# New planned times, a charge for changes to f32r products, and scores and transposes planned four at a time

## The chip, the cores and the metric

The kernel runs on one core of a Trainium2 chip. The metric is the device time of one execution in microseconds. A core has five engines that run side by side, each with its own queue of instructions: TensorE (PE: matrix products and transposes; PEld is its weight load), VectorE (DVE), ScalarE (ACT), GpSimd (POOL) and SyncE (SP, which here only starts DMAs). Each engine works through its queue in order; an instruction that has to wait for another engine holds up what is queued behind it.

## The reference

Three computations follow each other. The first is a gated linear attention with a complex decay over 768 steps, for 4 batches, 8 heads and 48 dimensions; the second a two-layer network with a leaky activation on the 3072 x 384 result; the third a mixture of 8 experts.

```
scale = min(mag, 0.999) / (mag + 1e-6)           # mag = |a|; a = a * scale
for t in range(768):                              # attention, per batch and head
    S = a[t][:, None] * S + k[t][:, None] * v[t][None, :]     # S complex, 48 x 48
    y[t] = q[t] @ real(S)
x = y as 3072 x 384
h = x @ w_in                                      # 384 -> 2048
g = max(h, 0) + alpha * min(h, 0)
x = g @ w_out                                     # 2048 -> 384
out = x                                           # where x @ w_skip <= 0
e = argmax(x @ w_gate); p = softmax(x @ w_gate)[e]            # elsewhere, 8 experts
out = x + p * (relu(x @ w1[e]) @ w2[e])           # 384 -> 1024 -> 384
```

## The kernel before

The sequence of tokens is cut into 24 sub-chunks of 128 tokens. For each sub-chunk `s`, `elementwise` (label `E`) normalises the decay on ScalarE and VectorE in tiles of 128x384 called X and Rr (logarithm, exponential, arctangent, sine, prefix scans), and writes the modulated q and k through DRAM into the tiles qh and kh. `attention` (label `P`) then makes on TensorE, in fp32:

- the scores at<-qh,kh, two groups of four heads (parts `a` and `b`), which VectorE masks into A;
- the transposes at<-ident,kh of kh, two groups of four (parts `t`, `u`), which ScalarE copies to kT;
- the outputs y<-A,vt and y<-qh,St (part `y`), the state update sps<-vt,kT (part `s`), which VectorE puts into St;
- the split of y into two f32r parts (part `h`): xhi, a cast on ScalarE, and xlo = y - xhi on VectorE.

`moe_block` (label `M`) takes two sub-chunks at a time, 256 tokens, so there are 12 blocks. Each has 8 pairs of hidden tiles: 18 products h<-xhi/xlo,wih/wil of 256 columns per pair; the activation hs; its parts gh (a cast on ScalarE) and gl (VectorE); and 12 products acc<-woh/wol,gh/gl of 394 columns. Products of f32r parts (hi x hi, hi x lo, lo x hi) stand for one fp32 product. The weights w_in and w_out come as 64-bit words and are decoded in the first 115 us (`decode`, labels `d`: raw, Ai and Ao on VectorE, then wih, wil, woh, wol). The second network's nine items (labels `I`, weights w1h, w1l, w2h, w2l) gather the tokens of an expert by DMA (xg), transpose them (xt<-ident,xg) and split them again into xhi and xlo before their h products. Filler products (h<-ident, fp32) keep TensorE busy between 27 and 55 us of the plan, where it waits.

The order is not the order of the code. Each operation is recorded in a `Plan` with an engine, a planned cost, what it reads and writes, and a planned time from the table `WHEN` (L55 on, tenths of a unit, one number for each operation of a label and part). `Plan.emit` then simulates the engines in time: on each engine it takes, of the operations that are ready in the simulation, the one with the lowest planned time, and adds its cost; the resulting order on each engine is what is emitted. It also places ScalarE's table loads (L1080), one for each change between the set of Ln/Exp and that of Arctan/Sin, and lets an operation of the loaded set go first if its planned time is within `stick` of the other. So a cost in the planner changes the order of everything behind it, and no instruction by itself.

In the trace, L1151 is `mm` (a single product), L1156 `transpose`, L1430 `columns` (a list of products planned as one operation), L1108 `act`, L1113 `copy`, L1120 `tt`, L1128 `stt`, L1139 `scan`. Before the change, the four scores of a group are four `mm` operations, and the four transposes are four `transpose` operations, each with its own planned time:

```
for x in range(4):
    mm(at[:, x * 128:(x + 1) * 128], kh[:, 4 * g + x, 0:128], qh[0:96, 4 * g + x, :], True, True)
```

Of the kernel before, what the change touches and what calls it, by code (L numbers as in the profile page):

```python
# [55 lines left out]
    "d": "764",  # L56
    "E0x": "28 237",
    "E0e": "191 90 98 104 146 172 122 58 111 168 179 168 176 89 100 175 178 190 213 191 200 204 217 165 229 238 "
        "312 177 217",
    "E0k": "179 283 281 403",  # L60
    "E0q": "502 478 626",
    "d0ir": "142",
    "d0i": "128 168 -3 28 -47",
    "d0or": "-301",
    "d0o": "256 265 332 397 409 661 496 285 458 269 458 453",
    "d1ir": "171",
    "d1i": "227 220 234 292 301",
    "d1or": "180",
    "d1o": "192 201 213 302 290 397 276 221 142 251 317 341",
    "E1x": "159 268",  # L70
    "E1e": "129 152 175 154 131 156 192 182 213 251 195 293 253 353 321 287 316 279 396 305 318 325 356 327 363 "
        "359 385 409 381",
    "E1k": "223 221 247 393",
    "E1q": "409 410 459",
    "P0v": "620",
    "P0a": "447 459 457 464 468",
    "P0b": "471 452 475 479 482",
    "P0t": "719 844 855 859 762",
    "P0u": "589 571 491 583 535",
    "P0y": "412",  # L80
    "P0s": "574 643",
    "P0h": "108 -31",
    "d2ir": "163",
    "d2i": "235 148 283 352 361",
    "d2or": "317",
    "d2o": "281 254 302 395 364 417 503 392 391 387 382 321",
    "d3ir": "272",
    "d3i": "24 -48 -81 -60 -36",
    "d3or": "208",
    "d3o": "347 355 360 275 429 364 360 386 475 272 288 269",  # L90
    "P1v": "290",
    "P1a": "376 425 296 307 315",
    "P1b": "490 478 481 479 491",
    "P1t": "639 638 662 773 609",
    "P1u": "764 769 873 804 837",
    "P1y": "741",
    "P1s": "628 973",
    "P1h": "481 497",
    "E2x": "247 288",
    "E2e": "343 295 299 393 394 484 436 520 459 427 462 491 470 544 385 491 561 563 645 592 569 589 620 697 624 "  # L100
        "716 708 724 719",
    "E2k": "665 720 490 777",
    "E2q": "828 747 894",
    "E3x": "447 919",
    "E3e": "384 490 455 398 539 664 586 589 588 600 642 669 658 655 732 736 759 830 881 777 825 835 852 893 862 "
        "891 877 902 906",
    "E3k": "961 949 876 961",
    "E3q": "798 648 808",
    "d4ir": "602",
    "d4i": "383 455 454 561 516",  # L110
    "d4or": "424",
    "d4o": "458 464 452 531 476 526 501 569 501 539 588 532 517",
    "d5ir": "-85",
    "d5i": "450 420 448 442 498",
    "d5or": "117",
    "d5o": "368 274 259 163 277 280 272 262 162 246 243 271 466",
    "d6ir": "481",
    "d6i": "557 562 538 605 598",
    "d6or": "859",
    "d6o": "499 508 541 572 506 562 651 626 625 392 385 431 563",  # L120
    "d7ir": "255",
    "d7i": "607 577 652 686 693",
    "d7or": "782",
    "d7o": "638 640 663 668 640 679 695 665 680 671 679 657 689",
    "d8ir": "340",
    "d8i": "670 686 600 709 673",
    "d8or": "508",
    "d8o": "667 707 683 741 732 729 678 685 725 743 752 746 728",
    "d9ir": "583",
    "d9i": "736 715 733 739 767",  # L130
    "d9or": "593",
    "d9o": "677 700 675 678 678 685 685 686 681 686 686 685 707",
    "P2v": "821",
    "P2a": "905 921 931 935 912",
    "P2b": "804 815 822 790 801",
    "P2t": "742 720 746 746 797",
    "P2u": "1013 1001 952 1015 1083",
    "P2y": "686",
    "P2s": "1098 1258",
    "P2h": "1061 1168",  # L140
    "d10ir": "853",
    "d10i": "745 764 770 774 835",
    "d10or": "619",
    "d10o": "819 811 825 854 834 862 877 863 883 893 918 896 935",
    "d11ir": "782",
    "d11i": "802 807 829 870 857",
    "d11or": "823",
    "d11o": "876 872 861 904 894 896 974 932 988 879 1041 940 899",
    "d12ir": "708",
    "d12i": "885 919 931 968 934",  # L150
    "d12or": "817",
    "d12o": "866 864 849 864 867 934 879 1055 968 1017 955 923",
    "P3v": "1119",
    "P3a": "1118 1088 1072 1047 1113",
    "P3b": "1057 1093 1056 1094 1124",
    "P3t": "1141 1142 1144 1143 1223",
    "P3u": "1079 1111 1114 1115 1141",
    "P3y": "810",
    "P3s": "1235 1610",
    "P3h": "1219 1172",  # L160
    "d13ir": "1157",
    "d13i": "966 1006 1003 869 815",
    "d13or": "1145",
    "d13o": "994 919 984 1029 1020 1017 924 1060 1083 1089 1075 895",
    "d14ir": "924",
    "d14i": "728 768 763 901 816",
    "d14or": "981",
    "d14o": "676 664 706 699 709 709 690 715 660 707 692 857",
    "d15ir": "946",
    "d15i": "1079 1084 1066 1132 1121",  # L170
    "d15or": "1535",
    "d15o": "1087 1069 1114 1111 1119 1112 1220 1166 1137 1174 1165 1167",
    "M0.0": "412 415 425 417 396 432 410 440 430 395 417 417 287 308 290 342 327 308 295 296 327 368 376",
    "M0.1": "617 643 664 651 675 659 646 656 650 614 668 597 674 674 690 707 699 699 712 713 704 724 748 668 702 "
        "750 710 720 679 808 720 744 738 766 768",
    "M0.2": "676 675 680 679 666 678 682 693 669 678 672 678 660 707 702 697 708 719 823 760 782 814 785 792 747 "
        "759 759 779 663 640 668 624 672 598 673",
    "M0.3": "696 617 667 720 717 580 616 589 601 616 639 650 647 633 654 658 637 658 674 713 634 712 728 653 655 "
        "627 658 664 677 659 689 696 677 695 739",
    "M0.4": "802 818 802 811 822 821 815 811 804 801 818 816 824 789 834 718 845 901 895 847 915 859 993 854 871 "  # L180
        "896 892 961 960 898 937 914 794 812 855",
    "M0.5": "849 845 849 833 849 855 823 871 900 879 885 877 879 865 886 910 886 885 992 955 959 1018 1016 989 "
        "1015 1018 992 975 962 1064 1020 1028 981 965 989",
    "M0.6": "973 998 985 1009 1004 976 1012 999 950 1017 952 993 1016 1044 1014 1005 1040 1020 1017 988 1023 1094 "
        "1054 1058 1001 969 968 984 1011 1054 1057 1023 1051 1070 1099",
    "M0.7": "1022 1035 1019 1048 1091 1047 1066 1068 1085 1112 1129 1091 1074 1061 1083 1108 1102 1118 1110 1123 "
# [24 lines left out]
    "E4k": "1335 1386 1217 1623",  # L211
    "E4q": "1286 1423 1381",
    "P4v": "1604",
    "P4a": "1469 1428 1430 1433 1444",
    "P4b": "1458 1405 1322 1316 1325",
    "P4t": "1529 1521 1540 1498 1508",
    "P4u": "1434 1435 1337 1297 1320",
# [2035 lines left out]
```

## Time and profile before

| | before |
|---|---|
| median of 3 runs | 747.38 us (747.15 to 749.46) |
| profiled execution | 749.78 us, of which the span of instructions is 747.8 us |
| TensorE busy | 703.7 us (94%), 7290 instructions |
| VectorE busy | 596.0 us (80%), 1401 instructions |
| ScalarE busy | 507.1 us (68%), 869 instructions, 83 of them profiled table loads of 1283 ns |
| GpSimd busy | 95.8 us (13%) |
| granted TensorE clock | 0.999 |

The span is 747.8 us; the rest of the execution lies around the first and last instruction. Busy shares over the span hide the stages: up to 60 us TensorE mostly waits for the decoded weights and the first attention outputs; from 60 to 617 us the first network's blocks and the attention of later sub-chunks share the engines; from 617 us the experts' items run; after 741 us only the last output is written. So each reading below is of one stretch. In a list of instructions in time, a record's duration is longer than the engine's time for it, since products are pipelined: the engine's time is the distance from one start to the next. A fp32 product shows as two records (x2), one for each of its passes.

### The profile page before, as it was taken

The numbers are of one execution on the slowest core, as the hardware profiler recorded it, in microseconds if no ns is written. First come the engines' busy times: TensorE is split into PE (matmuls) and PEld (weight loads), VectorE is DVE, ScalarE is ACT, GpSimd is POOL, SyncE is SP. The second block draws the span as 40 slices with busy tenths as digits, with TensorE's granted clock in tenths as the row PEclk, the third lists the DMA queues.
The fourth block names the chain that finished last, engine by engine and source line by source line (L and its number), as shares of the span: only waits on it lengthen the run. The fifth ranks groups of instructions, "written<-read, shape, count | busy, mean of one in ns | idle before, by whom it ended". The sixth has DMA issues, their size and how long they took to land.

```text
span 747.8 us, 18414 instructions
## 1 busy us (share of the span) xinstructions
PE 703.7 (94%) x7290; PEld 670.6 (90%) x7290; DVE 596.0 (80%) x1401; ACT 507.1 (68%) x869; POOL 95.8 (13%) x154
## 2 busy tenths in 40 slices
PE   0589999999999999999999999999999998999996
PEld 0478989889999999999989999999999998999996
DVE  7999999899988999899888899965465473886623
ACT  6779669799999888899889777632222362565411
POOL 5000000101201102010120100201010304502111
PEclk9999999999999999999999999999999999999999
DMA  8595862648654646365354957576543544799300
GB/s 292 157 288 191 265 204 72 150 136 234 168 136 117 205 131 181 105 179 172 95 125 143 244 175 229 159 185 190 154 138 118 162 157 145 243 396 396 118 16 19
DMA packets 84685, 130.64 MB, mean 175 GB/s; under 512 B 8822, under 2 KB 60096, under 8 KB 84592
## 3 DMA queue, kind: packets, MB, share of 16 engines
q1 hardware_dynamic: 79152, 111.19, 50.0%
q0 software_dynamic: 5440, 18.21, 7.8%
q8 instruction: 59, 0.97, 0.5%
q14 instruction: 34, 0.28, 0.1%
HBM read 99.46 MB, written 31.29 MB: 175 GB/s over the span
## 4 chain that ended last, share of the span: by engine, by line
PE 44%; DVE 17%; issue 14%; ACT 11%; DMA 10%; POOL 2%; SPq 1%; POOLq 0%; DVEq 0%; ACTq 0%
PE acc L1151 18%; PE h L1151 18%; ACT X L1108 4%; ACT L1080 4%; PE at L1151 3%; DVE X L1120 3%; PE y L1430 3%; DMA X<-in_a 3%; DVE X L1128 2%; DVE X L1139 2%; DMA raw<-in_w_out 2%; DMA qh<-qd 1%; DVE gl L1120 1%; DMA rawc<-in_w_out 1%; DMA lst<-tok,ix 1%
## 5 line engine op out<-in xcount | busy, mean ns | idle before, releaser
L1151 PE MATMUL h<-xhi,wih 128*128 128x256 f32 x576 | 163.0, 289 | 2.6 <-DVE hs L1120 1.2
L1151 PE MATMUL h<-xlo,wih 128*128 128x256 f32 x576 | 162.5, 286 | 0.2
L1151 PE MATMUL h<-xhi,wil 128*128 128x256 f32 x576 | 161.3, 285 | 0.0
L1108 ACT ACTIVATE X<-X 128x384 f32<-128x384 f32 (+1 forms) x216 | 119.0, 560 | 27.8 <-DVE X L1139 9.9
L1151 PE MATMUL acc<-woh,gh 128*128 128x394 f32 x384 | 134.1, 357 | 1.1 <-ACT gh L1113 1.1
L1151 PE MATMUL acc<-woh,gl 128*128 128x394 f32 x384 | 129.5, 348 | 1.3 <-DVE gl L1120 1.1
L1151 PE MATMUL acc<-wol,gh 128*128 128x394 f32 x384 | 129.8, 345 | 0.0
L1151 PEld LDWEIGHTS h<-xhi,wih 128*128 128x128 f32 x576 | 108.6, 190 | 5.9 <-ACT hs L1113 1.9
L1151 PEld LDWEIGHTS h<-xlo,wih 128*128 128x128 f32 x576 | 109.0, 190 | 1.2 <-DVE xlo L1120 0.9
L1151 PEld LDWEIGHTS h<-xhi,wil 128*128 128x128 f32 x576 | 108.9, 190 | 0.5 <-issue 0.4
L1080 ACT ACT_TABLE_LOAD x83 | 106.5, 1283 | 1.5
L1113 ACT CAST gh<-hs 128x512 fp32r<-128x512 f32 x96 | 58.3, 617 | 45.1 <-PE acc L1151 31.0
L1120 DVE TENSOR_TENSOR X<-X 128x384 f32<-128x384 f32 (+1 forms) x96 | 71.7, 750 | 13.4 <-ACT X L1108 12.9
L1120 DVE TENSOR_TENSOR gl<-hs,gh 128x512 fp32r<-128x512 f32 x96 | 65.0, 684 | 19.1 <-ACT gh L1113 18.7
L1151 PEld LDWEIGHTS acc<-woh,gh 128*128 128x128 f32 x384 | 71.6, 189 | 5.0 <-ACT gh L1113 3.0
L1128 DVE SCALAR_TENSOR_TENSOR hs<-hs,alp 128x256 f32<-128x256 f32 x144 | 62.1, 478 | 16.8 <-ACT hs L1113 16.6
L1151 PEld LDWEIGHTS acc<-woh,gl 128*128 128x128 f32 x384 | 71.6, 189 | 3.7 <-DVE gl L1120 2.9
L1151 PEld LDWEIGHTS acc<-wol,gh 128*128 128x128 f32 x384 | 72.5, 189 | 0.3 <-issue 0.2
L1113 ACT COPY hs<-h 128x512 f32<-128x512 f32 x72 | 40.1, 582 | 39.1 <-PE h L1151 33.4
L1612 POOL DMA_INDIRECT lst<-tok,ix x24 | 31.0, 1291 | 242.0 <-DVE ix L1124 227.7
L1151 PE MATMUL at<-qh,kh 96*128 96x128 f32 x384 | 54.6, 277 | 2.4 <-DMA qh<-qd 2.4
L1151 PEld LDWEIGHTS at<-qh,kh 96*128 96x128 f32 x384 | 49.8, 191 | 3.8 <-issue 2.2
(191 smaller groups left out, 1370.7 us busy)
## 6 DMA issues: line engine op xcount, KB each, us to landing
r<-in_w SPq DMA_DIRECT2D x24, 512.0 KB, 8.4
r<-in_w SPq DMA_DIRECT2D x32, 384.0 KB, 8.6
kd<-QP SPq DMA_DIRECT2D x24, 387.0 KB, 4.9
kh<-kd SPq DMA_DIRECT2D x24, 387.0 KB, 5.7
qd<-X SPq DMA_DIRECT2D x24, 384.0 KB, 3.2
qh<-qd SPq DMA_DIRECT2D x24, 384.0 KB, 5.0
X<-in_a POOLq DMA_DIRECT2D x18, 384.0 KB, 6.3
X<-in_qk POOLq DMA_DIRECT2D x18, 384.0 KB, 6.9
```

The source lines that it names most:

```text
L1080: nc.scalar.preload_act_table_set(o)
L1108: lambda: nc.scalar.activation(real(o), real(i), f, **{k: real(x) for k, x in kw.items()}),
L1113: lambda: nc.scalar.copy(real(o), real(i)), [i], [o])
L1120: dve(o, cols(o), lambda: nc.vector.tensor_tensor(out=real(o), in0=real(x), in1=real(y), op=op), [x, y], late=late)
L1128: dve(o, cols(o), lambda: nc.vector.scalar_tensor_tensor(out=real(o), in0=real(x), scalar=real(s), in1=real(y), op0=op0, op1=op1), [x, y, s])
L1139: dve(o, 2 * cols(o) - 16, lambda: nc.vector.tensor_tensor_scan(out=real(o), data0=real(x), data1=real(y), initial=real(init), op0=ALU.mul ...
L1151: pl.add("PE", cost / 1e3, lambda: nc.tensor.matmul(real(o), lhsT=real(l), rhs=real(r), start=start, stop=stop, skip_group_check=True), [l ...
L1430: ins = nc.tensor.matmul(real(o), lhsT=real(l), rhs=real(r), start=alone or first and n < 4, stop=alone or n >= len(ops) - 4, skip_group_c ...
L1612: r = nc.gpsimd.indirect_dma_start(out=lst, out_offset=bass.IndirectOffsetOnAxis(ap=real(ix[:, t:t + 1].bitcast(U32)), axis=0), in_=toks[t ...
```

## The change

Four things change, none of them in what is computed.

- An operation has a new field `swift`, true for f32r products (`mm` sets it). In the simulation of `Plan.emit`, a swift operation on TensorE that follows one that is not swift costs `swap` = 0.085 us more.
- The four scores of a group become one `columns` operation with a planned cost of 4 x 0.223 us, in place of four of their own.
- The four transposes of a group become one operation with a planned cost of 0.36 us.
- All numbers of `WHEN` are new; parts a, b, t and u have two numbers for each sub-chunk in place of five (four products and the operation behind them).

```
-    "P9a": "2306 2347 2382 2361 2409",
+    "P9a": "2371 2614",
...
-    def add(self, eng, cost, fn, reads=(), writes=(), after=(), lag=0.0, table=None, late=0.0):
+    def add(self, eng, cost, fn, reads=(), writes=(), after=(), lag=0.0, table=None, late=0.0, swift=False):
...
-        o.label, o.part = self.label, self.part
+        o.label, o.part, o.swift = self.label, self.part, swift
...
             if e == "PE":
+                cost += self.swap * (o.swift and not swift)
+                swift = o.swift
...
-    stick = 10
+    stick, swap = 10, 0.085
...
-               [l, r] + ([] if start else [o]), [o])
+               [l, r] + ([] if start else [o]), [o], swift=dt == F32R)
...
-                for x in range(4):
-                    mm(at[:, x * 128:(x + 1) * 128], kh[:, 4 * g + x, 0:128], qh[0:96, 4 * g + x, :], True, True)
+                columns([(at[:, x * 128:(x + 1) * 128], kh[:, 4 * g + x, 0:128], qh[0:96, 4 * g + x, :]) for x in range(4)],
+                        True, 4 * SCORE)
...
-                    for x in range(4):
-                        transpose(at[:, x * 96:x * 96 + 96], kh[:, 4 * g + x, 0:128], ident[0:96, 0:96])
+                    def turn(at=at, g=g):
+                        for x in range(4):
+                            ins = nc.tensor.transpose(real(at[:, x * 96:x * 96 + 96]), real(kh[:, 4 * g + x, 0:128]),
+                                                      ident[0:96, 0:96])
+                        return ins
+
+                    pl.add("PE", 0.36, turn, [kh[:, 4 * g:4 * g + 4, 0:128]], [at])
...
+        SCORE = 0.223
```

What this does to the order is shown at three places. After the change the lines are 4 higher for the helpers (L1155 for L1151, L1160 for L1156, and so on); scores and y stand at L1440, the grouped transposes at L1397. A row is one or more instructions of a queue in order; xN counts equal neighbours.

TensorE, the first group of scores of sub-chunk 9 (at<-qh_181,kh), among the products of the first network; before, single scores stand between products (from 238.8 us in the trace):

```order
L1151 MATMUL h<-xlo,wih 128x256
L1151 MATMUL at<-qh_181,kh 128x128
L1151 MATMUL acc<-woh,gh 128x394
L1151 MATMUL h<-xhi,wil 128x256
L1151 MATMUL h<-xhi,wih 128x256
L1151 MATMUL h<-xlo,wih 128x256
L1151 MATMUL h<-xhi,wil 128x256
L1151 MATMUL h<-xhi,wih 128x256
L1151 MATMUL at<-qh_181,kh 128x128
L1151 MATMUL h<-xlo,wih 128x256
L1151 MATMUL h<-xhi,wil 128x256
```

The same place after the change:

```order
L1155 MATMUL h<-xhi,wih 128x256
L1440 MATMUL at<-qh_181,kh 128x128 x4
L1440 MATMUL sps<-vt,kT 32x48 x24
L1440 MATMUL at<-qh_181,kh 128x128 x4
L1397 MATMUL at<-ident,kh 128x96 x4
L1155 MATMUL acc<-woh,gh 128x394
L1155 MATMUL h<-xlo,wih 128x256
```

The two groups of four scores now stand as two runs with one state update between them, and the transposes as a run of four directly behind.

VectorE around the second xlo<-y,xhi of the second block (block 1), which is the last thing that the block's products wait for. Rows of X and phc are steps of `elementwise`, Ao of `decode`, A the masked scores. Before:

```order
L1120 TENSOR_TENSOR hs<-h,hs 128x512
L1139 SCALAR_TENSOR_TENSOR X<-X,Rr 128x128 x3
L1120 TENSOR_TENSOR wol<-Ao,woh 128x384
L1120 TENSOR_TENSOR xlo<-y,xhi 128x3x128
L1120 TENSOR_TENSOR wol<-at,woh 128x10
L1120 TENSOR_TENSOR gl<-hs,gh 128x512
L1128 SCALAR_TENSOR_TENSOR X<-X 128x384
L1132 COPY chk<-X 128x3
L1120 TENSOR_TENSOR St<-sps,kh 96x8x48
L1120 TENSOR_TENSOR X<-X 128x384
L1128 SCALAR_TENSOR_TENSOR X<-X 128x384
L1120 TENSOR_TENSOR X<-X,Rr 128x2x384
```

After:

```order
L1136 COPY chk<-X 128x3
L1124 TENSOR_TENSOR X<-X 128x384
L1124 TENSOR_TENSOR A<-at,mask 128x512
L1132 SCALAR_TENSOR_TENSOR Ao<-raw,Ao 128x384
L1124 TENSOR_TENSOR X<-X 128x384
L1124 TENSOR_TENSOR A<-at,mask 128x512
L1132 SCALAR_TENSOR_TENSOR X<-X 128x384
L1124 TENSOR_TENSOR X<-X,phc 128x3
L1124 TENSOR_TENSOR X<-X,Rr 128x2x384
L1124 TENSOR_TENSOR X<-X 128x2x384
L1124 TENSOR_TENSOR hs<-h,hs 128x512
L1124 TENSOR_TENSOR xlo<-y,xhi 128x3x128
```

The steps chk, X<-X,Rr and X<-X of two times 384 columns, which stood behind this xlo, now stand ahead of it, as does hs; the copy of wol now stands behind it.

TensorE at the passage from the first network to the second, where xt<-ident,xg turns the first item's tokens and h<-xhi,w1h is the first product of an expert. Before:

```order
L1151 MATMUL acc<-wol,gh 128x394
L1151 MATMUL acc<-woh,gl 128x394
L1156 MATMUL xt<-ident,xg_8226 128x128 x6
L1151 MATMUL h<-xhi,w1h_8482 128x256
L1151 MATMUL h<-xhi,w1h_8453 128x256
L1151 MATMUL h<-xlo,w1h_8482 128x256
L1151 MATMUL h<-xhi,w1l_8532 128x256
```

After:

```order
L1155 MATMUL acc<-wol,gh 128x394 x2
L1160 MATMUL xt<-ident,xg_8255 128x128
L1155 MATMUL acc<-woh,gl 128x394
L1155 MATMUL acc<-woh,gh 128x394
L1155 MATMUL acc<-woh,gl 128x394
L1155 MATMUL acc<-woh,gh 128x394
L1155 MATMUL acc<-wol,gh 128x394
L1155 MATMUL acc<-woh,gl 128x394
L1155 MATMUL acc<-wol,gh 128x394
L1155 MATMUL acc<-woh,gl 128x394
L1155 MATMUL h<-xhi,w1h_8502 128x256
L1155 MATMUL h<-xlo,w1h_8502 128x256
```

Five of the six transposes have moved further ahead, and eight acc products of the last block's tail stand between the sixth and the first h product.

## Rows read from the trace of the kernel before

**Rows 1.** Busy us (instructions) per engine in stretches; then clock, DMA share, GB/s

```profile
60.00:115.00 55.00, 54.65 (x699) 48.90 (x700) 54.33 (x122) 41.65 (x94) 1.24 (x2) 1.00 0.69 205
113.66:188.36 74.70, 71.99 (x805) 67.93 (x801) 69.03 (x162) 67.50 (x124) 6.58 (x10) 1.00 0.58 154
115.00:200.00 85.00, 82.29 (x906) 77.75 (x906) 78.38 (x183) 77.74 (x142) 9.80 (x13) 1.00 0.57 150
150.00:200.00 50.00, 48.45 (x613) 45.72 (x605) 47.13 (x107) 47.78 (x85) 6.31 (x9) 1.00 0.62 171
200.00:540.00 340.00, 337.04 (x3713) 322.71 (x3712) 287.30 (x681) 259.93 (x415) 34.00 (x40) 1.00 0.59 165
```

**Rows 2.** Waits of PE, 200 to 540 us: us in total, times, longest

```profile
PE acc L1151 <- ACT gh L1113: 1.1, 3, 0.7
PE h L1151 <- ACT hs L1113: 1.1, 2, 0.7
```

**Rows 3.** PE in time: start, us, engine, line, operation, out<-in; scores among products

```profile
239.91 0.38 PE L1151 MATMUL at<-qh,kh 96*128 96x128 f32 x2
240.05 0.36 PE L1151 MATMUL h<-xlo,wih 128*128 128x256 f32 x1
240.25 0.28 PE L1151 MATMUL h<-xhi,wil 128*128 128x256 f32 x1
...
405.99 0.88 PE L1430 MATMUL sps<-vt,kT 128*32 128x48 f32 x48
...
407.14 1.95 PE L1151 MATMUL at<-qh,kh 96*128 96x128 f32 x16
...
409.05 0.28 PE L1151 MATMUL h<-xhi,wih 128*128 128x256 f32 x1
```

**Rows 4.** PE in time, single and grouped transposes of kh

```profile
117.46 0.25 PE L1156 MATMUL at<-ident,kh 96*128 96x96 f32 x1
117.49 0.36 PE L1151 MATMUL h<-xlo,wih 128*128 128x256 f32 x1
117.69 0.28 PE L1151 MATMUL h<-xhi,wil 128*128 128x256 f32 x1
117.81 0.41 PE L1156 MATMUL at<-ident,kh 96*128 96x96 f32 x3
118.00 0.43 PE L1151 MATMUL acc<-wol,gh 128*128 128x394 f32 x1
118.27 0.34 PE L1151 MATMUL acc<-woh,gl 128*128 128x394 f32 x1
118.45 0.34 PE L1151 MATMUL acc<-woh,gh 128*128 128x394 f32 x1
```

**Rows 5.** DVE: two instructions in time; then a group by shape, 15 to 115 us

```profile
114.95 0.55 DVE L1120 TENSOR_TENSOR xlo<-y,xhi 128x384 fp32r<-128x384 f32 x1
115.42 0.16 DVE L1120 TENSOR_TENSOR wol<-at,woh 128x10 fp32r<-128x10 f32 x1
...
L1120 DVE TENSOR_TENSOR X<-X,Rr 128x768 f32<-128x768 f32 x4 | 3.8, 948 | 0.0
```

**Rows 6.** ACT in time: the 8th and 20th gh, and a table load

```profile
113.66 0.62 ACT L1113 CAST gh<-hs 128x512 fp32r<-128x512 f32 x1
...
188.36 0.61 ACT L1113 CAST gh<-hs 128x512 fp32r<-128x512 f32 x1
...
208.26 1.28 ACT L1080 ACT_TABLE_LOAD   x1
209.56 0.52 ACT L1108 ACTIVATE X<-X 128x384 f32<-128x384 f32 x1
```

**Rows 7.** PE in time at the first item of the second network; brackets: idle before

```profile
617.40 0.82 PE L1156 MATMUL xt<-ident,xg 128*128 128x128 f32 x6
619.34 0.50 PE L1151 MATMUL h<-xhi,w1h 128*128 128x256 f32 x2 [1.12 <-ACT xhi L1113]
620.09 0.38 PE L1151 MATMUL h<-xlo,w1h 128*128 128x256 f32 x1 [0.26 <-DVE xlo L1120]
```

More of the change, by code (lines that the diff above doesn't have):

```diff
@@ L870 @@
 class Op:
-    __slots__ = ("eng", "cost", "lag", "fn", "pri", "seq", "table", "deps", "left", "users", "ready", "end", "sig", "label", "follow", "late", "part")
+    __slots__ = ("eng", "cost", "lag", "fn", "pri", "seq", "table", "deps", "left", "users", "ready", "end", "sig", "label", "follow", "swift", "late", "part")
 class Slots:
@@ L1001, in emit @@
                 heapq.heappush(waiting[o.eng], (0.0, o.seq, o))
-        table, order, now, dma, todo = None, [], 0.0, 0.0, len(self.ops)
+        table, order, now, dma, todo, swift = None, [], 0.0, 0.0, len(self.ops), False
         while todo:
```

1410 rows, old and new, of the table WHEN are left out of this document.

## The prediction

> **What bounds the kernel now.** I read the table of engine time by stretches first. From 60 us on TensorE is the limit: busy 54.65 of 55 us, then 82.29 of 85, then 337.04 of 340 [rows 1], and its clock is granted in full (1.00, the 2.4 GHz level). So the time falls only if TensorE gets less work, or if its waits shrink: 0.35, 2.71 and 2.96 us in these stretches. But TensorE is not alone: VectorE is busy 54.33 of 55 us up to 115 us [rows 1], so what VectorE is given before that mark moves everything behind it, and ScalarE reaches 47.78 of 50 us between 150 and 200 us [rows 1]. Last I read the waits of TensorE: from 200 to 540 us the two kinds that wait for ScalarE make up 2.2 us of the 2.96 [rows 2].
>
> No operation is added or removed. What changes is the order, in three ways: four scores, or four transposes of kh, now stand together; the planner charges 0.085 us for each f32r product that follows another kind; and every planned time is new. I therefore cost changes of kind first, then the moves.
>
> **Changes of kind: -0.9 us.** In the order of TensorE an f32r product follows another kind of operation 177 times before and 115 times after, 62 fewer; scores stand ahead of 52 of these before and 20 after, kh transposes ahead of 39 and 23. The price, from the trace: a single score starts at 239.91, and the second product behind it at 240.25 [rows 3]. Taking off one product's step of 0.12 leaves 0.22 us for the score. The run of eight scores goes from 407.14 to 409.05; less 0.12 this is 1.79 us, 0.224 each [rows 3]. So a score costs the same alone as in a run of eight. The product behind it does show 0.36 us in place of 0.28, but it starts early by as much: the lengthening is in the record and not in the spacing. Transposes: one takes 117.69 - 117.46 - 0.12 = 0.11 us, three take 118.27 - 117.81 - 0.18 = 0.28 [rows 4] (0.18 is the step of an acc product, 118.27 to 118.45). That is 0.085 each and 0.025 to 0.03 for each run. I take 0 for the 32 score runs that vanish and 0.03 for the 30 others: -0.9 us. The ends are 0, and 62 x 0.085 = -5.3 us if the lengthening were lost time everywhere. I stay near the first, since the rows measure the spacing itself.
>
> **The start: +3.0 us.** The mark is the second xlo of block 1, the last piece of x that this block's h products need; VectorE writes it at 114.95 [rows 5], and TensorE goes on with it at once. The VectorE order puts 241 instructions ahead of it before and 246 after. Items of 768 columns (0.948 us [rows 5]): two more. Items of 384 columns (0.55, as the xlo itself [rows 5]): 2 + 1 + 1 more and 2 + 1 fewer, net one more. Small ones (0.16): two more. Durations: 1.90 + 0.55 + 0.32 = 2.77 us. Neighbours overlap by 0.08 (114.95 + 0.55 against a start at 115.42 [rows 5]), and there are five more, so +2.35 us. Nothing hides it: VectorE has only 0.67 us idle in 55. The same count up to the first xlo of the kernel gives +2.1, so the delay is there from the first product on. SyncE's queue also has three more 384 KB weight loads ahead of the second sub-chunk's kh. I cost them at nothing, because VectorE is late there itself; without that cover they would lengthen the first wait.
>
> A late mark costs TensorE only what it can't do meanwhile. Between its first h product and the mark it has, after the change, three acc products and one identity product less (4 x 0.18), two transposes (0.17) and one fp32 product of 384 columns (as three scores, 0.67): 1.56 us less. In return one state update, sps (some 0.9 us by the row at 405.99 [rows 3]), is done before the first product. So about 0.65 us of work is pushed behind the mark: 2.35 + 0.65 = **+3.0**. The low end is 1.7, if VectorE's 0.67 us of idle time are used up and nothing is pushed behind; the high end is 4.5, if the delays of both marks add up.
>
> **ScalarE from 114 to 189 us: +1.0 us.** Ahead of the 20th gh cast (188.36 [rows 6]) ScalarE gets ten more instructions: four table loads (1.28 us, 208.26 [rows 6]), four activations of 384 columns (0.52, 209.56 [rows 6]) and two more of about 0.5. That is 8.2 us, of which 6.5 stand ahead of the 8th cast already (113.66 [rows 6]), where 13 us of idle time hide them (41.65 busy of 55 [rows 1]). Between the two casts (74.7 us) it was busy 67.5 us, or 90% [rows 1]; it will be 1.7 more, 69.2. TensorE's own work between its first uses of these two blocks of gh is 71.2 us in the new order, 4.0 less than before; with some 2.5 us of its other waits it wants the second 73.7 us after the first. ScalarE has to be busy 94% of that. It was 96% busy in the last 50 us before 200 [rows 1], but 90% over the stretch. At 96% the term is 0, at 90% it is 69.2 / 0.904 - 73.7 = 2.9 us; I take +1.0, nearer to the row of the same place, with -1 (another of its waits covered) and +3 as ends.
>
> The ScalarE load row ends when the next activation starts: 208.26 + 1.28 against 209.56 [rows 6]. The Trainium skill, "ScalarE: Activation LUTs", section "What ACT_TABLE_LOAD costs", says a drain of about 1.38 us comes with each load, 2.66 in all. By it the four loads would cost ScalarE another 5.5 us, an estimate, nearly all of it before 114 us where it is idle enough. The trace disagrees with the drain (0.02 us), and the sum goes by the trace.
>
> **Later waits: -0.8 us.** ScalarE has 74 table loads after and 84 before. Four more stand before 189 us, so 14 fewer behind it: 18 us less of the 260 that ScalarE is busy between 200 and 540 us [rows 1]. That should free part of the 2.2 us that TensorE waits for it there [rows 2]; I take a third. Ends: -2.2, and +3 if the new order brings as many new waits as there are now.
>
> **The passage to the second MoE: -1.4 us.** At 617.40 six transposes of x stand directly ahead of the first h product, which waits 1.12 us for ScalarE's xhi and then 0.26 for VectorE's xlo [rows 7]. In the new order five of the six come some hundred products earlier, and eight acc products stand between the last and the first h product: 8 x 0.18 = 1.44 us of work that covers the 1.38 us. Ends: -0.9 if the single late transpose is still felt, -2.3 if 0.9 us of the waits further on goes too.
>
> **Sum:** 3.0 + 1.0 - 0.8 - 0.9 - 1.4 = +0.9 us. The profiled execution took 749.78 us (span 747.8 and 1.98 around it); it would be 750.7. Against the median of 747.38 this is 748.3. The profiled one stands 2.4 above the median, and I assume that the terms carry over.
>
> **Rivals.**
> *ScalarE becomes the bound before 189 us (slower).* Mechanism: between the 8th and 20th gh cast ScalarE keeps the 90% of before, its 69.2 us take 76.6, and TensorE stands. It decides from a rate under 94%. Price 2.9 in place of 1.0: 750.2, more if VectorE, late too, lowers the rate further. For it: ScalarE's casts stand in line behind activations that wait for VectorE, busy 78.38 of 85 us there [rows 1]. Against it: the 96% row, and no wait of TensorE for a gh cast in that stretch.
> *The work done early is paid back (faster).* VectorE and ScalarE do more ahead of 115 us, so they have less to do behind it; then the 2.71 us of waits from 115 to 200 us go, the ScalarE term is nothing, and the whole 2.2 us of the later waits go: 748.3 - 1.0 - 2.7 - 1.4 = 743.2. For it: the moved items are the same ones, only earlier. Against it: a new order at these loads brings waits of its own.
> *The charge is real (faster).* If a change cost 0.085 us in spacing, 62 fewer give another -4.4: 743.9. Against it stand the two score readings, which agree within 0.01 us.
> That the change doesn't do what it says is out: the order has 62 fewer changes.
>
> **How the numbers follow.** About 0.3% (2.2 us) is what a measurement of this kernel can tell from no change: faster is under 745.1, slower above 749.6. The forecast of 748.3 has 0.42, of which 0.04 falls to slower and 0.01 to faster; ScalarE as the bound 0.25; paid back 0.22; the charge 0.08; the last 0.03 is some other middle result. Faster: 0.22 + 0.08 + 0.01 = 0.31. Slower: 0.25 + 0.04 = 0.29. The rest, 0.40, is no change. The forecast's own range by its terms is 745 to 752. The whole range reaches both neighbours: 743 to 753.
>
> **What would show it.** In the profile after: the second xlo of block 1 near 117.3 us and TensorE waiting just ahead of it; scores still 0.22 us apart, in runs of four; waits for gh or hs between 115 and 200 us of 2 to 5 us if ScalarE binds, and none if the work is paid back; the first h product of the second MoE without a wait over 0.3 us; the last 80 us as before. The prediction is wrong if the first h product comes as early as before, or if a stretch behind 200 us gains or loses more than 3 us.

## The result and the profile after

The changed kernel takes 751.04 us (median of 14 executions, 749.12 to 754.63) beside 747.55 us for the kernel before (14 executions): a ratio of 1.0052, 95% interval 1.0037 to 1.0067. It is slower by 2.8 to 5.0 us, where 0.9 us was forecast. The ratios, here and below, leave out the few executions that fell in a second, slower state; the medians don't. The profiled execution is the longest of the 14: 754.63 us, span 752.9. So what its rows explain is some 5 us, and the usual loss is 3.5.

The table of engine time by stretches, of the kernel after (us of the stretch, then the busy us of TensorE, its weight loads, VectorE, ScalarE and GpSimd, the granted clock, DMA share, GB/s):

```profile
15.00:60.00 45.00, 29.12 (x372) 25.14 (x372) 43.22 (x100) 33.86 (x70) 0.00 (x0) 0.96 0.78 226
60.00:115.00 55.00, 54.19 (x653) 48.02 (x654) 51.59 (x115) 40.11 (x89) 1.07 (x2) 0.94 0.70 202
61.00:67.00 6.00, 5.86 (x51) 4.80 (x51) 4.63 (x12) 1.91 (x5) 0.00 (x0) 0.50 0.19 53
115.00:200.00 85.00, 83.80 (x963) 79.25 (x964) 78.53 (x187) 79.98 (x142) 8.91 (x12) 1.00 0.52 142
200.00:540.00 340.00, 335.10 (x3708) 321.67 (x3707) 287.09 (x680) 245.28 (x408) 31.29 (x40) 1.00 0.58 167
```

Three things are new against [rows 1]. The clock isn't 1.00 throughout: from 61 to 67 us it is at 0.50, the 1.2 GHz level (and a first time from 34 to 37 us). VectorE, which was busy all but 0.67 us from 60 to 115 us, now stands 3.4 us there. And the idle time of TensorE from 115 us on is about what it was: 1.2 us up to 200 (2.71 before), 4.9 from there to 540 (2.96 before). So the loss is in the start. The list of TensorE in time shows it (start, us, then the instruction; the brackets give the idle time before it):

```profile
57.11 0.88 PE L1440 MATMUL sps<-vt,kT 128*32 128x48 f32 x48
59.98 2.86 PE L1440 MATMUL at<-qh,kh 96*128 96x128 f32 x16 [1.99 <-issue]
62.64 1.89 PE L1397 MATMUL at<-ident,kh 96*128 96x96 f32 x8
64.46 1.94 PE L1440 MATMUL y<-A,vt 128*32 128x128 f32 x32
...
67.86 0.49 PE L1155 MATMUL h<-xhi,wih 128*128 128x256 f32 x2
```

The scores of the second sub-chunk start at 59.98 us; before they started at 55.48. Two idle microseconds stand ahead of them, and after these the clock falls: the run of eight scores takes 2.86 us where a run of eight took 1.95 in [rows 3]. The first h product comes at 67.86 us, 7.1 later than before (60.75): 4.5 us because the scores start late, and 2.6 because the stretch from them to that product takes 7.9 us in place of 5.3. VectorE and SyncE tell why the scores are late. VectorE of the kernel after, around the modulated k (QP) of that sub-chunk:

```profile
41.34 0.96 DVE L1124 TENSOR_TENSOR X<-X,Rr 128x768 f32<-128x768 f32 x1
43.50 0.36 DVE L1128 TENSOR_SCALAR Ao<-raw 128x384 int32<-128x384 int32 x1 [1.20 <-PE at L1440]
43.78 0.55 DVE L1124 TENSOR_TENSOR wil<-Ai,wih 128x384 fp32r<-128x384 f32 x1
44.24 0.95 DVE L1124 TENSOR_TENSOR X<-X 128x768 f32<-128x768 f32 x1
45.11 0.55 DVE L1132 SCALAR_TENSOR_TENSOR Ao<-raw,Ao 128x384 int32<-128x384 int32 x1
45.58 0.16 DVE L1124 TENSOR_TENSOR wol<-at,woh 128x10 fp32r<-128x10 f32 x1
45.66 0.95 DVE L1124 TENSOR_TENSOR QP<-X 128x768 f32<-128x768 f32 x1
```

SyncE's queue of the kernel after (the duration is that of the issue, not of the transfer):

```profile
46.64 0.38 SPq L1360 DMA_DIRECT2D kd<-QP  x1
47.12 0.54 SPq L1164 DMA_DIRECT2D raw<-in_w_in  x1
48.10 0.33 SPq L1362 DMA_DIRECT2D qh<-qd  x1
48.48 0.43 SPq L1164 DMA_DIRECT2D X<-in_a  x1
48.96 0.42 SPq L1164 DMA_DIRECT2D X<-in_qk  x1
51.47 0.33 SPq L1362 DMA_DIRECT2D kh<-kd  x1
```

In the kernel before QP started at 39.31. Here it starts at 45.66, behind a decode step that waits 1.2 us for TensorE and behind the q product. The store kd goes out as QP ends, at 46.64, and lands 4.8 us later; only then does the load kh go out, at 51.47, behind a weight load, qh and two X loads. It lands 8.4 us later, at 59.9, and the scores start at 59.98 (the last figure of the row is the time from issue to landing):

```profile
kh<-kd SPq DMA_DIRECT2D x1, 387.0 KB, 8.4
```

The mark that the prediction used, the second xlo of block 1, moved from 114.95 [rows 5] to

```profile
121.55 0.54 DVE L1124 TENSOR_TENSOR xlo<-y,xhi 128x384 fp32r<-128x384 f32 x1
```

which is 6.6 us later, and the first product of the second network comes at 624.4 us (619.3 before). The last product starts at 746.03 (740.65). TensorE did not stand at the mark: it is busy all of the 6.55 us ahead of it, and idle only 0.66 us between its first h product and the mark. So what the start costs TensorE has been lost by its first h product.

```profile
115.00:121.55 6.55, 6.55 (x95) 5.77 (x95) 6.55 (x15) 6.52 (x13) 0.00 (x0) 1.00 0.03 11
```

### The profile page after: what moved, and what is told of

Its sections match the earlier page's. It is cut to its first block, busy times and chain, and to the rows that moved or that the text cites. A ratio compares the mean times of both kernels' runs of the same rounds, so it can differ in the third digit from the quotient of the medians.

```text
span 752.9 us, 18376 instructions
## 1 busy us (share of the span) xinstructions
PE 709.1 (94%) x7286; PEld 676.3 (90%) x7286; DVE 593.9 (79%) x1401; ACT 492.3 (65%) x859; POOL 92.2 (12%) x154
## 4 chain that ended last, share of the span: by engine, by line
PE 44%; DVE 6%; ACT 3%; issue 1%; POOL 0%; POOLq 0%; ACTq 0%
PE acc L1155 20%; PE h L1155 20%; PE y L1440 2%; PE at L1440 2%; DVE X L1124 1%; DVE hs L1132 1%; ACT X L1112 1%; ACT L1084 1%; DVE X L1132 1%; DVE gl L1124 1%; DVE X L1143 1%; PE xt L1160 1%; PE at L1397 0%; ACT Rr L1112 0%; PE sps L1440 0%
## 5 line engine op out<-in xcount | busy, mean ns | idle before, releaser
L1155 PE MATMUL h<-xhi,wih 128*128 128x256 f32 x576 | 163.6, 289 | 1.4 <-DVE hs L1124 1.0
L1155 PE MATMUL h<-xlo,wih 128*128 128x256 f32 x576 | 162.8, 285 | 0.1
L1155 PE MATMUL h<-xhi,wil 128*128 128x256 f32 x576 | 161.6, 283 | 0.0
L1155 PE MATMUL acc<-woh,gh 128*128 128x394 f32 x384 | 133.2, 353 | 0.5 <-ACT gh L1117 0.3
L1155 PE MATMUL acc<-wol,gh 128*128 128x394 f32 x384 | 130.0, 343 | 0.0
L1155 PE MATMUL acc<-woh,gl 128*128 128x394 f32 x384 | 129.2, 347 | 0.0
L1155 PEld LDWEIGHTS h<-xhi,wih 128*128 128x128 f32 x576 | 108.6, 190 | 5.7 <-DVE hs L1124 1.7
L1155 PEld LDWEIGHTS h<-xlo,wih 128*128 128x128 f32 x576 | 109.4, 190 | 0.6 <-DVE xlo L1124 0.3
L1155 PEld LDWEIGHTS h<-xhi,wil 128*128 128x128 f32 x576 | 109.3, 190 | 0.1
L1155 PEld LDWEIGHTS acc<-woh,gh 128*128 128x128 f32 x384 | 71.8, 189 | 3.9 <-ACT gh L1117 1.9
L1155 PEld LDWEIGHTS acc<-woh,gl 128*128 128x128 f32 x384 | 71.7, 188 | 2.2 <-DVE gl L1124 0.9
L1155 PEld LDWEIGHTS acc<-wol,gh 128*128 128x128 f32 x384 | 72.6, 189 | 0.2
L1623 POOL DMA_INDIRECT lst<-tok,ix x24 | 27.9, 1161 | 268.4 <-DVE ix L1128 221.8
L1440 PE MATMUL at<-qh,kh 96*128 96x128 f32 x384 | 50.5, 281 | 3.6 <-issue 2.0
L1132 DVE SCALAR_TENSOR_TENSOR X<-X 128x384 f32<-128x384 f32 x96 | 52.4, 552 | 0.0
```

The source lines that it names most:

```text
L1132: dve(o, cols(o), lambda: nc.vector.scalar_tensor_tensor(out=real(o), in0=real(x), scalar=real(s), in1=real(y), op0=op0, op1=op1), [x, y, s])
L1155: pl.add("PE", cost / 1e3, lambda: nc.tensor.matmul(real(o), lhsT=real(l), rhs=real(r), start=start, stop=stop, skip_group_check=True), [l ...
L1440: ins = nc.tensor.matmul(real(o), lhsT=real(l), rhs=real(r), start=alone or first and n < 4, stop=alone or n >= len(ops) - 4, skip_group_c ...
L1623: r = nc.gpsimd.indirect_dma_start(out=lst, out_offset=bass.IndirectOffsetOnAxis(ap=real(ix[:, t:t + 1].bitcast(U32)), axis=0), in_=toks[t ...
```

## The experiments

Ratios are to the kernel before, run on the same chip in between; the chips differ, so a time is read only against those beside it.

**Fillers ahead of the late scores.** Ten filler products, in the changed kernel:

```
+  if o.label == "P1" and o.part in ("a", "b") and o.eng == "PE" and not warm:
+      warm.append(o)
+      for _ in range(10):
+          self.filler()
   o.fn()
```

> The changed kernel with ten filler products put on TensorE directly ahead of the scores of the second sub-chunk, where the profile after shows 2 us of idle time and then a granted clock of 0.50 from about 61 to 67 us. Nothing else is changed. Theory 1 (the low clock is part of the loss): the clock stays at 1.00 there, the scores, transposes and y of the second sub-chunk take about 2.6 us less, the first h product comes at about 65.2 us in place of 67.9, and the kernel takes 2 to 3 us less than the changed kernel, 748.5, or 1.001 of before. Theory 2 (the stretch is bound by VectorE and the loads, the clock costs nothing): first h product at 67 to 68 us, 751 us, 1.005 of before.

752.25 us, 1.0045 (1.0026 to 1.0063). The fall at 61 to 67 us is gone, yet the first h product comes at 66.7, between the two theories: in this execution QP started at 46.83, 1.2 us later than in the profile after, and the clock was at 0.50 from 33 to 39 us (34 to 37 in the profile after), after an idle gap at 30 to 34. The second xlo of block 1 came at 122.8. Theory 2 by the time; but one low stretch went and the other grew.

**The start of before in the changed kernel.** The rows of `WHEN` for E0 to E3, P0, P1, all of d and M0 are those of before (two numbers of five kept for the grouped parts).

> The changed kernel with the planned times of before for the start alone: elementwise of sub-chunks 0 to 3, attention of 0 and 1, all of decode, and the first block of products. Grouping, the charge and all other times are those of the changed kernel. Theory 1 (the start makes the whole loss, and the later order gains some 2 us of it back): first h product at 60 to 61 us as before, no low clock, and 745 to 746 us, 0.997 to 0.998 of before. Theory 2 (the later order only caught up because the start was late): 747 to 748 us, 1.000. Theory 3 (the loss is in the later order): 750 us or more, 1.004.

759.58 us, 1.0147 (1.0098 to 1.0195), so slower than either kernel. Theories 1 and 2 missed; theory 3's bound of 750 us is met, its 1.004 is not. The start was that of before, with the first h product at 60.7 us, but the first product of the third block came at 173.7 (166.0 before, 172.3 after). The clock was at 0.50 from 107 to 110 us. Between 60 and 200 us TensorE stood 8.7 us, and its waits were of many kinds:

```profile
PE h L974 <- DVE hs L943: 3.5, 2, 2.1
PE h L974 <- ACT wih L936: 1.0, 1, 1.0
PE acc L974 <- DVE gl L943: 0.8, 1, 0.8
PE at L1259 <- ACT wt L936: 0.7, 1, 0.7
```

A table of planned times is one piece: the rows behind a start are fitted to it. This says nothing on the start by itself.

**A f32r product between any two scores.** For each run of four scores, up to three f32r products that stand a little later and are ready are emitted between them:

```
+  ...                                 # near: up to three such products
+  for k, f in enumerate(o.bits):      # the four scores
+      f()
+      if k < len(near):               # f32r products pulled forward
+          near[k].fn()
```

> The changed kernel with each run of four scores broken up: a f32r product that stands a little later on TensorE and is ready is pulled between two scores, up to three per group. TensorE's order then has 230 changes to f32r in place of 115; the other engines' orders stay. Theory 1 (a change costs nothing in spacing for scores): 751 us, within 0.2% of the changed kernel, 1.005 of before. Theory 2 (the planner's 0.085 us is lost time): 115 x 0.085 = 9.8 us more, 761 us, 1.018 of before.

762.62 us, 1.0143 (1.0104 to 1.0182). By its total this looks like theory 2, whose 9.8 us would give 1.018. The rows say otherwise. TensorE of this kernel in time:

```profile
209.86 0.39 PE L1233 MATMUL at<-qh,kh 96*128 96x128 f32 x2
210.00 0.36 PE L999 MATMUL h<-xlo,wih 128*128 128x256 f32 x1
210.20 0.38 PE L1233 MATMUL at<-qh,kh 96*128 96x128 f32 x2
210.34 0.36 PE L999 MATMUL h<-xhi,wil 128*128 128x256 f32 x1
210.54 0.39 PE L1233 MATMUL at<-qh,kh 96*128 96x128 f32 x2
```

A score and a product together take 210.20 - 209.86 = 0.34 us: 0.22 for a score as in [rows 3] and 0.12 for a product, with a change at each. The product lasts 0.36, and begins 0.08 early. From the first product of the seventh block to the last product, where the clock is 1.00 in both, this kernel has 42 more changes than the changed one; the busy time of TensorE there (first row this kernel, second row the changed one) is

```profile
374.80:753.20 378.40, 376.28 (x3314) 367.39 (x3311) 258.75 (x630) 187.09 (x315) 52.83 (x58) 1.00 0.56 172
```

```profile
369.20:746.00 376.80, 375.66 (x3316) 367.18 (x3311) 258.67 (x630) 186.96 (x315) 55.21 (x58) 1.00 0.55 173
```

0.6 us more, or 0.015 us per change; the whole stretch is 1.6 us longer, waits included, or 0.04 per change at most; the charge would be 3.6. So theory 1 holds for the spacing. Most of the other extra time goes with a low clock: five of its six executions go from 754.1 us (mean clock 0.996) to 763.0 (0.989), and in the profiled one the clock was low from 60 to 71 us (61 to 67 in the profile after) and again from 265 to 269. Why this kernel falls there more often isn't settled, and the changed kernel did not run beside it.

**Grouping alone.** All planned times of before, `swap = 0`, each group at the latest time of its four.

> The kernel before with scores and transposes planned four at a time, each group at the latest planned time of its four, without the charge and with all other planned times of before. Changes to f32r on TensorE: 143 in place of 177. Theory 1 (grouping by itself is nearly free): 746 to 748 us, 0.998 to 1.001 of before, first h product near 61 us. Theory 2 (each change avoided saves 0.085 us): 2.9 us less, 744.6, 0.996. A result over 749 would say that grouping itself costs waits for the masked scores.

751.86 us, 1.0040 (1.0024 to 1.0055): over 749, the case that was put last. From 60 to 200 us the grouped kernel's TensorE is idle 7.4 us (3.1 before), and the waits named first are

```profile
PE h L974 <- ACT xhi L936: 1.9, 1, 1.9
PE acc L974 <- ACT gh L936: 1.8, 1, 1.8
```

The profiled execution, at a clock of 0.999, made this up by its end (last product at 740.7, as before; 748.99 us), while the five others, at 0.992 to 0.996, took 751.4 to 753.6. So grouping moves waits into the first 200 us by itself, whatever the new times are, mostly for ScalarE's casts and less for the masked scores (0.9 us); but the execution with a trace lost nothing by them. What the other five lost isn't seen in a trace. The 34 changes saved bring no visible gain.

**Fillers in all three gaps.** 16, 9 and 10 filler products ahead of the three waiting operations.

> The changed kernel with filler products in all three of its idle gaps on TensorE before the first h product: 16 ahead of the third decode's transposes (3.1 us idle, after which the granted clock was 0.50 from 34 to 37 us), 9 ahead of the product that waited 1.7 us at 47.1, and 10 ahead of the second sub-chunk's scores. The run with the last ten alone was no faster; there the clock still fell at 32 to 40 us. Theory 1 (the low clock ahead of 70 us costs the end of the kernel): clock 0.998 or more, first h product near 65 us, 747 to 749 us, 0.998 to 1.000 of before. Theory 2 (VectorE and ScalarE bind what follows, so the clock there is nearly free): clock up, time 750 to 752, 1.004.

758.29 us, 1.0052 (1.0029 to 1.0075). The clock stayed at 1.00 up to 640 us and the first h product came at 64.7, as theory 1 has it; but the second xlo of block 1 came at 120.0, only 1.5 us earlier than in the profile after, and the second network began at 623.0, 1.4 earlier. The ratio is near theory 2: by it TensorE's clock in the start is worth little as long as VectorE's work is late. But the time is no clean test. On this chip a wait ahead of the second item's products (h<-xf,r) came in, 5.9 us here and 3.8 in the kernel before with fillers; with it the clock fell here (646 to 653 us), and the executions have mean clocks of 0.992 to 0.997, hardly higher than those of the changed kernel (0.988 to 0.996).

**The late k moved forward.** In the emitted order of the changed kernel one VectorE instruction and two DMA issues move, and nothing else:

```
+  _, prod, kd, kh = [x for x in self.ops if x.label == "E1" and x.part == "k" and x.eng != "NONE"]
+  place(prod)               # QP: directly behind what it needs
+  place(kd)
+  ...                       # sp: places of SyncE's operations ahead of kh
+  place(kh, sp[-2])         # ahead of the two X loads
```

> The changed kernel with one VectorE instruction and two DMA issues moved: QP of the second sub-chunk (its modulated k) stands directly behind X<-X,Rr and ahead of the decode step Ao that waited 1.2 us for TensorE; its store kd stands ahead of qd, and its load kh ahead of the two loads of X for a later sub-chunk. In the profile after, QP ended at 46.6 us against 40.3 before, and the scores that need it came 4.5 us later. Theory 1 (this late k is what makes the start late): QP at 42.7, scores of the second sub-chunk near 57 us, no 2 us gap and no low clock at 61 to 67, first h product near 63 to 64 us, and 747 to 749 us, 0.999 of before. Theory 2 (the second xlo of block 1 is set by all of VectorE's work, so only the gap moves): first h product earlier, second xlo of block 1 still at 120 to 122 us, 750 to 752, 1.004.

Median 757.69 us, 1.0019 (0.9985 to 1.0053), on the chip of the run above. First h product at 62.9, second xlo at 117.1, second network at 620.9: 5.0, 4.4 and 3.5 us earlier than in the profile after. From 645 us on short waits among the h<-xf,r products and one of 2.1 us for gh followed, and the clock fell (648 to 655). Theory 1 by the marks; the interval was too wide to decide.

**The kernel before with fillers in its gaps.**

> The kernel before, order unchanged, with filler products in its own four gaps ahead of 56 us (16, 5, 3 and 3). Its profile shows the clock at 1.00 but its other executions have mean clocks of 0.995 to 0.999 and 748 to 752 us. Theory 1 (the executions differ by clock falls in the start): all executions at 0.999, spread under 1 us, median 1 to 2 us lower, 0.998. Theory 2 (they differ by when the loads arrive): spread and median as before, 1.000.

755.59 us, 1.0016 (0.9989 to 1.0044). The mean clocks were 0.992 to 0.998, no better than those of before beside it. Theory 2: the executions differ by something else too; in the one profiled here it was the wait ahead of h<-xf,r at 640 to 644 us.

**The new start with the old rest.** The rows exchanged the other way, with grouping and `swap = 0`.

> The counterpart of the run with the old start: scores and transposes planned four at a time with all planned times of before, as in the run with grouping alone, but the planned times of the start (elementwise of sub-chunks 0 to 3, attention of 0 and 1, decode, the first block) are those of the changed kernel. Theory 1 (the new start is what loses): first h product at 67 to 68 us, and 3 to 6 us slower than grouping alone, 755 to 758 us, 1.008 to 1.012 of before. Theory 2 (the new start is harmless, waits behind it absorb it): within 0.2% of grouping alone, 1.004.

762.13 us, 1.0102 (1.0068 to 1.0135), as theory 1 has it in time; but not for its reason. The first h product came at 62.9 us, and then TensorE stood 6.8 us between 60 and 115 us, 3.2 of it for VectorE's wol. QP started at 44.32 and the scores at 57.64, with 0.45 us of idle time ahead of them, so the gap that the late k makes isn't in this run. As with the old start, the two parts of a table don't fit each other.

**Control, and the late k again beside it.**

> The changed kernel again, unaltered, as the control for the three below on the same chip. All theories: 1.004 to 1.006 of before, first h product at 67 to 68 us, second xlo of block 1 at 121 to 122 us.

755.46 us, 1.0064 (1.0037 to 1.0091): the loss is there again. The marks are later than expected, first h product at 69.6 us and second xlo at 129.3; the profiled execution is the longest of the ten, and its clock was at 0.50 three times (33 to 39, 63 to 70 and 115 to 121 us).

> The kernel of the run with the early k of the second sub-chunk again, beside the changed kernel on the same chip; in its first run a wait for the second item's weights at 645 to 654 us, which the kernel before showed there too, hid what had been gained by 620 us (3.5 us against the profile after). Theory 1 (the late k is most of the loss): 3 to 4 us less than the changed kernel beside it, 0.999 to 1.001 of before. Theory 2 (a gain at 620 us is lost again behind it): within 1 us of the changed kernel, 1.004.

750.44 us, 1.0013 (0.9992 to 1.0035): under the unaltered kernel beside it by 4.5 us (754.97, its median without the longest execution) and by 0.5% in the ratios, whose intervals just don't touch. Theory 1. TensorE and VectorE of this kernel in time, to be read against the rows of after above:

```profile
44.05 0.96 DVE L956 TENSOR_TENSOR QP<-X 128x768 f32<-128x768 f32 x1 [1.68 <-ACT X L944]
```

```profile
57.13 0.88 PE L1272 MATMUL sps<-vt,kT 128*32 128x48 f32 x48
57.95 2.05 PE L1272 MATMUL at<-qh,kh 96*128 96x128 f32 x16
...
62.51 1.08 PE L1272 MATMUL y<-A,vt 128*32 128x128 f32 x32
...
64.36 0.49 PE L987 MATMUL h<-xhi,wih 128*128 128x256 f32 x2
```

QP gains only 1.6 us, since it now waits 1.68 us for ScalarE. Of these only 0.6 reach the load: kh now stands behind qh, which waits for its own store, and goes out at 50.91 (51.47 after). The larger gain is the transfer itself, now ahead of the two X loads:

```profile
kh<-kd SPq DMA_DIRECT2D x1, 387.0 KB, 6.4
```

It takes 6.4 us in place of 8.4, and 4.8 and 6.0 in the two runs below, where it stands ahead of them too (7.4 with the order of after and fillers). kh lands 2.6 us earlier, at 57.3. That is enough: the scores follow sps without a gap, the clock holds there, scores take 2.05 in place of 2.86 us and y 1.08 in place of 1.94, and the first h product is 3.5 us earlier. The second xlo comes at 118.7, the second network at 620.7, the last product 3.2 us earlier than in the profile after. No run moves one of the three instructions alone.

**Both sub-chunks' k.**

> As the run above, and the same done for the first sub-chunk: its QP (ended at 31.4 us in the profile after against 27.4 before) stands directly behind the steps it needs, its store and load kd and kh follow at once. Theory 1 (the lateness of k adds up over both sub-chunks): scores of the first sub-chunk near 46 us in place of 49.6, first h product near 61 to 62 us, another 1 to 2 us less than the run above, 0.997 to 0.999 of before. Theory 2 (VectorE's other work now sets the first product): first h product at 62 to 63 us, same time as the run above.

751.48 us, 1.0037 (1.0014 to 1.0061); first h product at 64.0, second xlo at 118.5. Theory 2 by the marks, though the time is no better than above: the first sub-chunk's k was not what waited.

**Both, with fillers ahead of 50 us.**

> The run above with 16 filler products ahead of the third decode's transposes and 6 ahead of the product that waited at 47.1 us, so that the granted clock doesn't fall at 34 to 38 us. Theory 1 (the low clock there still costs): 1 to 2 us less than the run above, mean clock 0.998 or more. Theory 2 (the clock of fillers and transposes there is nearly free, as in the run with more fillers): within 0.5 us of it.

750.49 us, 1.0010 (0.9992 to 1.0028), mean clock 0.998. That is 1.0 us under the run above, with mean clocks of 0.996 to 0.999 (0.991 to 0.997 above): the size of theory 1. But first h product and second xlo are those of the run above to 0.1 us, so the fillers gained nothing there; in the profiled execution the waits for VectorE's masked scores A were 1.4 us (3.0 above) and that for kh of 1.3 us was gone, and the last product came at 740.5 (742.96 above), where before it was at 740.65. How fillers ahead of 50 us would bring that about isn't shown. The intervals of the last three overlap. None beats the kernel before.

## Why the forecast was too low

The time lies in the range, and its sign is that of the sum, but the likeliest case was "no change" (0.40, against 0.29 for slower), and the kernel is slower by more than that. Term by term:

- **Changes of kind (-0.9).** The step from the rows was right: the charge of 0.085 us is a longer record and no longer spacing. In the run with 115 more changes a score takes 0.22 us between products, and a change 0.015 us (0.04 at most). The rival that rested on the charge is out. Whether grouping saves the 0.9 us can't be seen by itself.
- **The start (+3.0): the step that failed.** The count of instructions ahead of the mark was right (241 and 246), and its price nearly: VectorE is busy 2.5 us longer up to the mark. But the mark moved by 6.6 and not by 2.35 us. The sentence "Nothing hides it" took VectorE as busy all the time, before and after. In the profile after it stands 5.2 us between 15 and 115 us (45 - 43.22 and 55 - 51.59), where it stood 1.1 before, 4.1 more: 2.5 + 4.1 = 6.6. The row of before that [rows 1] lacks, and VectorE's longest wait in the kernel after from 60 to 115 us:

```profile
15.00:60.00 45.00, 29.65 (x426) 25.94 (x427) 44.56 (x103) 35.12 (x69) 0.00 (x0) 1.00 0.76 227
DVE A L1124 <- PE at L1440: 2.5, 2, 1.7
```

What it waits for are mostly scores that come late and slowly. In the four profiles with the early k it stands 1.0 to 2.6 us from 15 us up to the mark. The other sentence that failed stands beside it: loads ahead of the second sub-chunk's kh were costed at nothing "because VectorE is late there itself". It was also misread: in the queues of the two profiles two more weight loads stand ahead of kh and not three, but also qh and the two X loads. The place of QP in VectorE's order had no term at all. The run with the early k prices that place and the two X loads together: 3.2 us at the last product in the profiles, 4.5 by the medians. And the sign "TensorE waiting just ahead of it" did not come: the time was lost ahead of the first h product, 7.1 us, and not at the mark.
- **The clock** was not in the sum at all. Before, it held at 1.00 from 60 us on; the profile after shows it at half for 6 us behind a gap that the late k makes. In the profiles it is worth less than it looks: fillers that kept it up ahead of 640 us brought the first h product forward by 3.2 us and the second network by 1.4. What it is worth in the medians stays open: the mean clock of the 14 executions is 0.988 to 0.996 (0.993 to 0.999 for the kernel before beside the control), and no run held it up throughout in the changed order and left the late k as it is.
- **ScalarE to 189 us (+1.0)** came out at or below nothing: between the 8th and the 20th gh cast, at 121.66 and 196.00 us, it was busy 69.5 us (69.2 forecast) of 74.3, or 93%, and TensorE had no wait for gh from 115 to 200. The rival in which ScalarE binds is out; that its price of 750.2 us lies close to the measured time is luck.
- **Later waits (-0.8)** came out at +1.9 (4.9 us against 2.96), inside its ends. ScalarE's share fell as forecast; new waits took its place, for masked scores and kh, of the kernel after from 200 to 540 us:

```profile
PE at L1397 <- DVE A L1124: 2.5, 3, 1.2
PE at L1440 <- DMA kh<-kd: 0.8, 1, 0.8
PE at L1440 <- ACT kT L1117: 0.6, 1, 0.6
PE acc L1155 <- ACT gh L1117: 0.3, 1, 0.3
```

- **The passage (-1.4)** was right: the first item waits for nothing. It lost 0.6 us again at xf, further on.

That the moved work is paid back later, the other rival, holds in part: 7.1 us at the first h product were 5.1 at the second network. The marks of eleven profiles show how far the start decides:

| kernel | second xlo of block 1 | first product of the second network |
|---|---|---|
| before | 114.95 | 619.3 |
| before, with fillers | 115.8 | 621.6 |
| early k, first run | 117.1 | 620.9 |
| both k, with fillers | 118.5 | 618.9 |
| both k | 118.5 | 621.2 |
| early k, again | 118.7 | 620.7 |
| grouping alone | 119.3 | 619.9 |
| fillers in three gaps | 120.0 | 623.0 |
| after | 121.55 | 624.4 |
| fillers ahead of the late scores | 122.8 | 623.5 |
| after, control (its longest execution) | 129.3 | 632.5 |

A later mark goes with a later second network, but only to within 2 or 3 us: the two runs with both k have the same mark and differ by 2.3 behind it, and grouping alone has a late mark and an early second network. Such differences between single executions are not much smaller than the loss of 3.5 us, so the share of the late k rests on the medians of the two kernels run side by side, more than on these marks.

What stays open is how much of the 3.5 us is grouping. Grouping alone measured 0.4% slower, for a reason that its one profile doesn't show (that execution is as fast as before), and it can't be added to the late k.

## What to carry to other kernels

When a moved step feeds a transfer that feeds the first work of the bounding engine, follow it through every queue to that work, and ask what goes out ahead of it there. A count of instructions ahead of a mark holds only while the engine that is counted does not start to wait; check what its next instructions wait for in the new order. A longer record behind a change of operation is not a cost until the distance between starts is longer too. And a table of planned times can't be tested by exchanging part of it; move single instructions in the emitted order instead.

## What the runs showed of the hardware

In the kernel after, the clock of TensorE fell to 0.50 twice in the start and stayed there though TensorE was busy again: from 34 to 37 us, behind an idle gap of 3.12 us, and from 61 to 67 us, where a gap of 1.99 us had ended at 59.98. From 54 to 60 us TensorE was busy 3.66 us:

```profile
54.00:60.00 6.00, 3.66 (x89) 2.73 (x87) 5.46 (x11) 5.97 (x14) 0.00 (x0) 1.00 1.04 331
```

The Trainium skill, "TensorE: Matmul & The Clock Gate", section "HAM oscillation — how this bites in real kernels", describes the same: a wait for a DMA makes the engine idle long enough to be throttled, and the next work starts cold. The rows agree in kind (kh landed at 59.9, the scores started at 59.98, and the clock fell within the next 1.1 us).

By the one profile with fillers in three gaps, the cold stretches cost the second network only 1.4 us, where VectorE is late as well.

A record of 1.00 early in an execution doesn't prove the full clock. The same three transposes, in the kernel before (first two rows) and after (last two), where the record reads 1.00, 1.00, 0.50 and 1.00:

```profile
28.55 0.87 PE L1156 MATMUL at<-ident,Ao 128*128 128x128 f32 x3 [3.56 <-DVE Ao L1128]
35.64 0.52 PE L1156 MATMUL at<-ident,Ao 128*128 128x128 f32 x3
33.88 0.87 PE L1160 MATMUL at<-ident,Ao 128*128 128x128 f32 x3 [3.12 <-DVE wol L1124]
41.11 0.52 PE L1160 MATMUL at<-ident,Ao 128*128 128x128 f32 x3 [0.26 <-DVE wol L1124]
```

The first took as long as the third, which speaks for the lower pace there too. The wait ahead of the second item's products h<-xf,r, none over 0.6 us in the profiles of before and after and 3.8 and 5.9 us in two of the four profiles taken on one chip, was not expected either.
